# Attention with spatial reduction, then a gated feed-forward layer: a reordered prologue with larger loads, weights cast by DMA and dummy products

## Chip, cores and metric

One NeuronCore of a Trainium2 chip. The metric is device microseconds of one execution. Each kernel was run several times, with one execution profiled; the median of the runs is given.

Words used: TensorE (PE) multiplies, DVE is VectorE, ACT is ScalarE, POOL is GpSimd, SP is SyncE, which issues most loads. PEld is TensorE's loading of weights. PSUM is the memory that TensorE's products are written to; this kernel uses it in eight banks. SBUF is the memory in which the other tiles lie.

## The reference

```python
# q [4, 12288, 128], kv [4, 384, 32, 128], w_sr [128, 128]; float32
kv_pool = kv.reshape(B, H//4, 4, W//4, 4, C).mean(axis=(2, 4))   # 768 rows per image
k = v = kv_pool.reshape(B, -1, C) @ w_sr
s = (q @ k.transpose(0, 2, 1)) / sqrt(C)
a = exp(s - max);  a /= a.sum(-1, keepdims=True) + 1e-9
x = (a @ v).reshape(49152, 128)
out = (np.maximum(x @ w_gate, 0.0) * (x @ w_val)) @ w_out        # 1536 wide
```

Each of the four images gives 768 pooled rows: six **chunks** of 128. A chunk is pooled (adds over 4 lines, then over 4 columns), turned, projected by `w_sr` to keys, and turned once more to serve as values. The 49152 queries go through in 96 **tiles** of 512.

## The kernel before

The main loop runs, in one iteration, the scores of tile k, the values of tile k-1, the feed-forward products of tile k-3 and the output product of tile k-4. The keys of images 1 to 3 are made inside it, with GpSimd doing the adds. Only the first image has nothing to hide behind: its keys are made in a **prologue**, with the scores of the first four tiles beside them. These are the parts concerned.

```python
def pool_lines(eng, b, jc, other=None):             # chunk jc: 4 lines -> 1
    parts = kv_in.pop((b, jc))
    ...
    for i in range(2):                              # i == 0 on GpSimd in the prologue
        (other if i == 0 and other else eng).tensor_tensor(
            s2[:, i], parts[:, 2 * i], parts[:, 2 * i + 1], op=ALU.add)
    eng.tensor_tensor(s1, s2[:, 0], s2[:, 1], op=ALU.add)
    return s1
...
def values(k, jc, half, turn=True):
    ...                                             # 2 products of 128 x 129 (column 128: the sum)
    if jc == NJC - 1:
        ...                                         # own: the columns of this half
        nc.vector.tensor_copy(x16s[k][:, own, :], x_ps[:, :, 0:C])
        nc.vector.reciprocal(rinvs[k][:, own], x_ps[:, :, C])
        if half == 1:                               # inverse squares, used on the output
            ...                                     # rinv: the four inverses of the tile
            nc.vector.tensor_tensor(inv2s[k][:, :, 0], rinv, rinv, op=ALU.mult)
...
# prologue
for pair in range(1, NJC // 2):
    kv_load(0, pair, fine=pair == NJC // 2 - 1)     # last pair in 2 KB pieces
... # float32 weights loaded by SyncE into staging tiles
for jc in range(NJC):
    s1 = pool_lines(nc.vector, 0, jc, nc.gpsimd)
    kvT = turn_pooled(s1)                           # 4 float32 turns summed in PSUM, copy by DVE
    ...                                             # values of tile 0, chunk jc-1
    project(0, jc, kvT)                             # float32 product, copy by DVE: the keys
    ...                                             # values of tile 1, chunk jc-1
    for k in range(GRP):
        scores(k, jc)                               # product, exponential by ACT
        if k == 0:
            turn_values(0, jc)
q_load(1); q_turn(1)
for w16, w32 in staged:
    nc.gpsimd.tensor_copy(w16, w32)                 # weights cast by GpSimd
q_load(2)
...                                                 # last values of tiles 0 and 1, turn of tile 0
for k in range(LAG, last + 1):                      # main loop
    ...
```

The softmax here doesn't subtract the row's maximum and nothing guards it: scores larger than these inputs give would overflow.

## Time and profile before

| | kernel before |
|---|---|
| median of 4 runs | 1066.1 us (1065.6 to 1069.05) |
| profiled span | 1064.3 us |
| prologue, to the first feed-forward product | 46.93 us |
| first main iteration, to the first output product | 8.19 us |
| an undisturbed later tile (from its first output product to the next tile's) | 10.52 us |

The prologue is short, so averages over the span hide it. One has to cut the trace at its landmarks: the first score product of each chunk, the first feed-forward product (where TensorE becomes full), and the first output product. The prediction below does so. Two groups, with shapes kept apart, show that something disturbs the adds (columns: line, engine, operation, tiles, shapes, count, then busy us and mean ns, then idle before):

```profile
L140 DVE TENSOR_TENSOR s<-parts 128x512 f32<-128x512 f32 x6 | 6.8, 1127 | 3.6 <-DMA parts<-in_kv_dram 3.6
...
L144 DVE TENSOR_TENSOR s<-s 128x512 f32<-128x512 f32 x6 | 5.3, 883 | 0.6
```

An add of this shape takes 0.69 us when nothing disturbs it; a mean of 1127 ns over six means that some took far longer.

### The profile page before, as it was taken

What the parts mean: (1) busy time and instruction counts of PE and PEld (TensorE: products, weight loads), DVE (VectorE), ACT (ScalarE), POOL (GpSimd) and SP (SyncE); (2) the same over time, 40 slices, a digit from 0 to 9 for tenths busy, and PEclk for the clock granted to TensorE, in tenths of its full rate; (3) what the DMA queues carried; (4) which work ended last, traced back from release to release, by engine and by line L of the source; (5) the groups of instructions that cost most, each with busy time, mean ns of one, the idle gap of its engine ahead of it and who ended that gap; (6) DMA issues with size and microseconds to landing.
All of it is one profiled execution on the core that took longest, in us unless ns stands there. A gap on an engine that the chain in (4) does not pass through costs nothing.

```text
span 1064.3 us, 26131 instructions
## 1 busy us (share of the span) xinstructions
PE 1033.3 (97%) x9930; PEld 687.2 (65%) x9930; DVE 929.6 (87%) x1816; ACT 910.2 (86%) x1746; POOL 114.8 (11%) x132
## 2 busy tenths in 40 slices
PE   4699999999999999999999999999999999999997
PEld 2366666666666666666666666666666666666664
DVE  3698989998989898989898989898989898988896
ACT  3498888888888888888888888888888888888886
POOL 2200033300000004520000001530000000000000
PEclk9999999999999999999999999999999999999999
DMA  9631446422413325523132235552322332313121
GB/s 295 152 75 31 85 130 171 123 55 62 86 30 86 66 76 182 157 58 86 31 85 59 57 71 130 145 144 51 85 61 55 71 63 54 66 36 61 42 35 45
DMA packets 126574, 91.93 MB, mean 86 GB/s; under 512 B 101872, under 2 KB 103536, under 8 KB 126448
## 3 DMA queue, kind: packets, MB, share of 16 engines
q1 hardware_dynamic: 123136, 78.21, 27.7%
q0 software_dynamic: 3312, 12.06, 6.8%
q8 instruction: 77, 1.26, 0.5%
q14 instruction: 49, 0.40, 0.1%
HBM read 52.76 MB, written 25.17 MB: 73 GB/s over the span
## 4 chain that ended last, share of the span: by engine, by line
PE 96%; DVE 2%; DMA 1%; issue 0%; ACT 0%; SPq 0%; ACTq 0%; DVEq 0%
PE bank_ps L253 24%; PE bank_ps L239 23%; PE bank_ps L228 23%; PE bank_ps L198 12%; PE bank_ps L186 11%; PE bank_ps L168 1%; PE bank_ps L158 1%; DMA parts<-in_kv_dram 1%; DVE s L140 1%; DVE s L144 1%; DVE hT L242 0%; SPq L134 0%; ACT o_sb L263 0%; PE bank_ps L175 0%; DVE x L205 0%
## 5 line engine op out<-in xcount | busy, mean ns | idle before, releaser
L242 DVE SCALAR_TENSOR_TENSOR hT<-bank_ps,val 128x512 f16<-128x512 f32 x1152 | 765.2, 687 | 100.2 <-ACT val L232 70.0
L232 ACT CAST val<-bank_ps 128x512 f16<-128x512 f32 x1152 | 678.1, 589 | 120.4 <-PE bank_ps L228 117.9
L253 PEld LDWEIGHTS <-hT 128*128 128x128 f16 x4608 | 351.1, 98 | 206.0 <-DVE hT L242 2.9
L253 PE MATMUL bank_ps<-wo,hT 128*128 128x128 f16 x4608 | 443.4, 219 | 2.1 <-DVE hT L242 2.0
L228 PE MATMUL bank_ps<-xT,wv 128*128 128x512 f16 x1152 | 436.6, 379 | 1.3 <-DVE xT L223 1.3
L239 PE MATMUL bank_ps<-xT,wg 128*128 128x512 f16 x1152 | 435.7, 378 | 0.9 <-DVE hT L242 0.9
L187 ACT ACTIVATE aT<-bank_ps 128x512 f16<-128x512 f32 x576 | 345.4, 603 | 17.5 <-PE bank_ps L186 17.5
L198 PE MATMUL bank_ps<-kv,aT 128*128 128x129 f16 x2304 | 225.8, 220 | 0.1
L198 PEld LDWEIGHTS <-aT 128*128 128x128 f16 x2304 | 178.7, 98 | 70.1 <-issue 1.5
L186 PE MATMUL bank_ps<-qT,kv 128*128 128x512 f16 x576 | 217.6, 382 | 0.5 <-DVE kv L169 0.5
L239 PEld LDWEIGHTS <-wg 128*128 128x128 f16 x1152 | 111.4, 97 | 65.1
L228 PEld LDWEIGHTS <-wv 128*128 128x128 f16 x1152 | 112.7, 98 | 0.1
L205 DVE CAST x<-bank_ps 128x256 f16<-128x256 f32 x192 | 79.6, 415 | 0.7 <-PE bank_ps L198 0.7
L77 POOL DMA_DIRECT2D q<-in_q_dram x23 | 12.6, 546 | 553.6 <-DMA qT<-q 553.4
L140 POOL TENSOR_TENSOR s<-parts 128x512 f32<-128x512 f32 x42 | 52.9, 1269 | 168.1 <-DMA parts<-in_kv_dram 159.8
L265 DVE TENSOR_TENSOR o_sb<-bank_ps,inv 128x512 f32<-128x512 f32 x93 | 63.3, 681 | 0.0
L186 PEld LDWEIGHTS <-kv 128*128 128x128 f16 x576 | 56.5, 99 | 3.7 <-issue 1.6
L206 DVE RECIPROCAL rinv<-bank_ps 128x2 f32<-128x2 f32 x192 | 30.7, 160 | 0.0
L158 PE MATMUL bank_ps<-ident,s 128*128 128x128 f32 x42 | 10.0, 317 | 14.2 <-DVE s L144 14.2
L144 POOL TENSOR_TENSOR s<-s 128x512 f32<-128x512 f32 x18 | 22.8, 1268 | 1.4
L210 DVE TENSOR_TENSOR inv<-rinv 128x4 f32<-128x4 f32 x96 | 18.2, 190 | 3.3
L158 PEld LDWEIGHTS bank_ps<-ident,s 128*128 128x128 f32 x42 | 5.8, 159 | 17.3 <-DVE s L144 5.9
(33 smaller groups left out, 101.4 us busy)
## 6 DMA issues: line engine op xcount, KB each, us to landing
out_dram<-o_sb SPq DMA_DIRECT2D x96, 256.0 KB, 2.2
parts<-in_kv_dram SPq DMA_DIRECT2D x44, 512.0 KB, 6.1
q<-in_q_dram POOLq DMA_DIRECT2D x23, 512.0 KB, 5.1
parts<-in_kv_dram SPq DMA_DIRECT2D x8, 256.0 KB, 9.7
xT<-x SPq DMA_TRANSPOSE x94, 2.5
q<-in_q_dram SPq DMA_DIRECT2D x4, 256.0 KB, 7.7
w<-in_moe_w_val_dram SPq DMA_DIRECT2D x2, 384.0 KB, 7.6
w<-in_moe_w_gate_dram SPq DMA_DIRECT2D x2, 384.0 KB, 7.7
```

Source lines behind the costliest of these rows:

```text
L140: (other if i == 0 and other else eng).tensor_tensor(s2[:, i], parts[:, 2 * i], parts[:, 2 * i + 1], op=ALU.add)
L144: eng.tensor_tensor(s1, s2[:, 0], s2[:, 1], op=ALU.add)
L186: nc.tensor.matmul(s_ps, kv16[:, k // NST, jc, 0:C], qT_of(k), start=True, stop=True)
L187: nc.scalar.activation(aTs[k][:, jc, :], s_ps, AF.Exp, scale=qk_scale)
L198: nc.tensor.matmul(x_ps[:, i, :], aTs[k][:, jc, s * 128 : (s + 1) * 128], kv16[:, k // NST, jc, C : 2 * C + 1], start=(jc == 0 and i == 0) ...
L205: nc.vector.tensor_copy(x16s[k][:, own, :], x_ps[:, :, 0:C])
L228: nc.tensor.matmul(va_ps, wv16[:, fb * 128 : (fb + 1) * 128], xTs[k], start=True, stop=True)
L232: nc.scalar.copy(val, va_ps)
L239: nc.tensor.matmul(g_ps, wg16[:, fb * 128 : (fb + 1) * 128], xTs[k], start=True, stop=True)
L242: nc.vector.scalar_tensor_tensor(hTs[k][:, fb, :], g_ps, 0.0, vals.pop((k, fb)), op0=ALU.max, op1=ALU.mult)
L253: nc.tensor.matmul(o_ps[:, s, :], hTs[k][:, fb, s * 128 : (s + 1) * 128], wo16[:, fb, :], start=(fb == 0 and s == 0), stop=(fb == NFB - 1) ...
L265: nc.vector.tensor_tensor(o_sb, o_ps, inv2.to_broadcast([128, NS, 128]), op=ALU.mult)
```

## The change

Its intent is to shorten the prologue. All pieces of the first image are 4 KB; chunk jc+1 is pooled, turned and projected while the scores of chunk jc run; DVE does nearly all adds; weights come as float16 by a casting DMA; 34 dummy products run before and 34 after the first q turn, to bring TensorE to its full clock; five pairs of the value products of tile 2 move from the first main iteration into the prologue's waits, and some copies move to ScalarE.

```diff
-def kv_load(b, pair, fine=False):          # 2 KB pieces where fine
+def kv_load(b, pair):                      # 4 KB pieces (two chunks side by side)
 ...
-    staged: float32 weights by SyncE, cast later by nc.gpsimd.tensor_copy
+    idle = bank([128, 128])
+    def keep_warm(n):
+        for _ in range(n):
+            nc.tensor.matmul(idle, ident16, ident16, start=True, stop=True)
+    keep_warm(34)
     q_cast(0)
     q_turn_pe(0)
+    keep_warm(34)
 ...
+    (chunk 0: adds, turns, projection, keys; chunk 1: adds; q turns 1 to 3)
     for jc in range(NJC):
-        (adds, turns, projection, keys of chunk jc, then scores of tiles 0 to 3)
+        scores(0, jc)
+        turn_values(0, jc, nc.scalar.copy)
+        turn_pooled(0, jc + 1, ...)         # if there is one
+        for k in range(1, GRP):
+            scores(k, jc)
+        project(0, jc + 1)
+        keep_keys(0, jc + 1)
+        # even jc: four adds, for chunks jc+2 and jc+3 (one of chunk 4's on GpSimd);
+        # odd jc: the two adds left of chunk jc+2, around keep_keys
+        (values of tiles 0 and 1, chunk jc-1)
+        if jc == 2:
+            for own in (slice(0, D_FF // 2), slice(D_FF // 2, D_FF)):
+                nc.gpsimd.dma_start(wv16[:, own], moe_w_val[:, own])
+                nc.gpsimd.dma_start(wg16[:, own], moe_w_gate[:, own])
+            q_load(1); q_turn(1)
+            nc.gpsimd.dma_start(wo16, moe_w_out.rearrange("(fb f) c -> f fb c", f=128))
+            q_load(2)
+    (values of tile 2, half 0, chunks 0 to 4, ahead of the first turn of x)
```

More of the change, by code (lines that the diff above doesn't have):

```diff
@@ L88, in q_turn, with q_load_plain @@
         qTs[g] = qT
-    def q_load_plain(i):
-        q32 = work.tile([128, NS, C], FP32, tag="q32", bufs=GRP, name="q32")
+    def q_load_plain(i0, i1):
+        q32 = work.tile([128, i1 - i0, NS, C], FP32, tag=f"q32_{i0}", bufs=1, name="q32")
         nc.sync.dma_start(
-            q32, q[0, 0 : GRP * T, :].rearrange("(p i s) c -> i p s c", p=128, i=GRP)[i]
+            q32, q[0, 0 : GRP * T, :].rearrange("(p i s) c -> p i s c", p=128, i=GRP)[:, i0:i1]
         )
-        q32s[i] = q32
+        for i in range(i0, i1):
+            q32s[i] = q32[:, i - i0]
     def q_cast(i):
@@ L118, with add_lines @@
     kv_in = {}
-    def kv_load(b, pair, fine=False):
+    def kv_load(b, pair):
         parts = work.tile([128, r, 2, r, C], FP32, tag="kv_in", bufs=3)
-        lines = kv[b, pair * 2 * HC : (pair + 1) * 2 * HC]
+        rows = kv[b, pair * 2 * HC : (pair + 1) * 2 * HC].rearrange(
+            "(hp dh) (wp h dw) c -> dh hp wp (h dw c)", dh=r, h=2, dw=r
+        )
+        for dh in range(r):
+            nc.sync.dma_start(parts[:, dh].rearrange("p h dw c -> p (h dw c)"), rows[dh])
         for h in range(2):
             kv_in[b, 2 * pair + h] = parts[:, :, h]
-            rows = lines[h * HC : (h + 1) * HC].rearrange(
-                "(hp dh) (wp dw) c -> dh hp wp (dw c)", dh=r, dw=r
-            )
-            for dh in range(r if fine else 0):
-                nc.sync.dma_start(parts[:, dh, h].rearrange("p dw c -> p (dw c)"), rows[dh])
-        rows = lines.rearrange(
-            "(hp dh) (wp h dw) c -> dh hp wp (h dw c)", dh=r, h=2, dw=r
-        )
-        for dh in range(0 if fine else r):
-            nc.sync.dma_start(parts[:, dh].rearrange("p h dw c -> p (h dw c)"), rows[dh])
-    def pool_lines(eng, b, jc, other=None):
-        parts = kv_in.pop((b, jc))
-        s2 = work.tile([128, 2, r, C], FP32, tag="kv_s2")
-        for i in range(2):
-            (other if i == 0 and other else eng).tensor_tensor(
-                s2[:, i], parts[:, 2 * i], parts[:, 2 * i + 1], op=ALU.add
-            )
-        s1 = work.tile([128, r, C], FP32, tag="kv_s1")
-        eng.tensor_tensor(s1, s2[:, 0], s2[:, 1], op=ALU.add)
-        return s1
+    s2s, s1s, kv_Ts, key_banks = {}, {}, {}, {}
+    def add_lines(eng, b, jc, i):
+        if i == 0:
+            s2s[b, jc] = work.tile([128, 2, r, C], FP32, tag="kv_s2", bufs=2, name="kv_s2")
+        parts, s2 = kv_in[b, jc], s2s[b, jc]
+        if i < 2:
+            eng.tensor_tensor(s2[:, i], parts[:, 2 * i], parts[:, 2 * i + 1], op=ALU.add)
+        else:
+            s1s[b, jc] = work.tile([128, r, C], FP32, tag="kv_s1", bufs=2, name="kv_s1")
+            eng.tensor_tensor(s1s[b, jc], s2[:, 0], s2[:, 1], op=ALU.add)
+            del kv_in[b, jc], s2s[b, jc]
     def pool_columns(eng, s1):
@@ L152, in pool_columns, with turn_pooled @@
         return s3
-    def turn_pooled(pooled):
+    def turn_pooled(b, jc, pooled):
         tp = bank([128, 128])
@@ L161, in turn_pooled, with project, keep_keys, turn_values @@
             )
-        kvT = work.tile([128, 128], FP32, tag="kvT")
-        nc.vector.tensor_copy(kvT, tp)
-        return kvT
-    def project(b, jc, kvT):
-        pr = bank([128, 128])
-        nc.tensor.matmul(pr, w_sr_f32, kvT, start=True, stop=True)
+        kv_Ts[b, jc] = work.tile([128, 128], FP32, tag="kvT", name="kvT")
+        nc.vector.tensor_copy(kv_Ts[b, jc], tp)
+    def project(b, jc):
+        key_banks[b, jc] = bank([128, 128])
+        nc.tensor.matmul(key_banks[b, jc], w_sr_f32, kv_Ts.pop((b, jc)), start=True, stop=True)
+    def keep_keys(b, jc):
         nc.vector.tensor_scalar(
-            kv16[:, b, jc, 0:C], pr, 1.0 / (r * r), None, op0=ALU.mult
+            kv16[:, b, jc, 0:C], key_banks.pop((b, jc)), 1.0 / (r * r), None, op0=ALU.mult
         )
-    def turn_values(b, jc):
+    def turn_values(b, jc, copy):
         vt = bank([128, 128], FP16)
         nc.tensor.transpose(vt, kv16[:, b, jc, 0:C], ident16)
-        nc.vector.tensor_copy(kv16[:, b, jc, C : 2 * C], vt)
+        copy(kv16[:, b, jc, C : 2 * C], vt)
     aTs, x_banks, x16s, xTs, rinvs, inv2s = {}, {}, {}, {}, {}, {}
@@ L187, in scores, with values @@
         nc.scalar.activation(aTs[k][:, jc, :], s_ps, AF.Exp, scale=qk_scale)
-    def values(k, jc, half, turn=True):
+    def values(k, jc, half):
         if jc == 0:
@@ L202, in values, with keep_values, x_turn @@
             )
-        if jc == NJC - 1:
-            own = slice(2 * half, 2 * half + 2)
-            nc.vector.tensor_copy(x16s[k][:, own, :], x_ps[:, :, 0:C])
-            nc.vector.reciprocal(rinvs[k][:, own], x_ps[:, :, C])
-            if half == 1:
-                rinv = rinvs.pop(k)
-                inv2s[k] = work.tile([128, NS, 1], FP32, tag="inv2", bufs=8, name="inv2")
-                nc.vector.tensor_tensor(inv2s[k][:, :, 0], rinv, rinv, op=ALU.mult)
-            if half == 1 and turn:
-                x16 = x16s.pop(k)
-                xT = work.tile([128, NS, 128], FP16, tag="xT", bufs=5, name="xT")
-                nc.sync.dma_start_transpose(xT, x16.rearrange("p s c -> p (s c)"))
-                xTs[k] = xT.rearrange("c s p -> c (s p)")
+    def keep_values(k, half, copy=nc.vector.tensor_copy):
+        own = slice(2 * half, 2 * half + 2)
+        x_ps = x_banks.pop((k, half))
+        copy(x16s[k][:, own, :], x_ps[:, :, 0:C])
+        nc.vector.reciprocal(rinvs[k][:, own], x_ps[:, :, C])
+        if half == 1:
+            rinv = rinvs.pop(k)
+            inv2s[k] = work.tile([128, NS, 1], FP32, tag="inv2", bufs=8, name="inv2")
+            nc.vector.tensor_tensor(inv2s[k][:, :, 0], rinv, rinv, op=ALU.mult)
+    def x_turn(k):
+        x16 = x16s.pop(k)
+        xT = work.tile([128, NS, 128], FP16, tag="xT", bufs=5, name="xT")
+        nc.sync.dma_start_transpose(xT, x16.rearrange("p s c -> p (s c)"))
+        xTs[k] = xT.rearrange("c s p -> c (s p)")
     def x_turn_pe(k):
@@ L287 @@
     nc.sync.dma_start(w_sr_f32, w_sr)
-    q_load_plain(0)
+    q_load_plain(0, 1)
     kv_load(0, 0)
-    for i in range(1, GRP):
-        q_load_plain(i)
+    q_load_plain(1, GRP)
     for pair in range(1, NJC // 2):
-        kv_load(0, pair, fine=pair == NJC // 2 - 1)
+        kv_load(0, pair)
     wg16 = const.tile([128, D_FF], FP16)
@@ L297 @@
     wo16 = const.tile([128, NFB, 128], FP16)
-    HF = D_FF // 2
-    staged = []
-    w32 = work.tile([128, 2, 2, HF], FP32, tag="kv_in", bufs=3, name="w32")
-    for i in range(2):
-        own = slice(i * HF, (i + 1) * HF)
-        for n, (w16, w) in enumerate(((wv16, moe_w_val), (wg16, moe_w_gate))):
-            nc.sync.dma_start(w32[:, i, n], w[:, own])
-            staged.append((w16[:, own], w32[:, i, n]))
-    w32 = work.tile([128, NFB, 128], FP32, tag="kv_in", bufs=3, name="w32")
-    nc.sync.dma_start(w32, moe_w_out.rearrange("(fb f) c -> f fb c", f=128))
@@ L308, with pool_of @@
-    staged.append((wo16, w32))
+    def pool_of(jc):
+        return nc.gpsimd if jc == NJC - 2 else nc.vector
+    idle = bank([128, 128])
[3 more added lines that the diff above has]
+    keep_warm(34)
     q_cast(0)
     q_turn_pe(0)
-    for jc in range(NJC):
-        s1 = pool_lines(nc.vector, 0, jc, nc.gpsimd)
-        kvT = turn_pooled(s1)
-        if jc == 0:
-            for i in range(1, GRP):
-                q_cast(i)
-        else:
-            values(0, jc - 1, 0, turn=False)
-            values(0, jc - 1, 1, turn=False)
-        project(0, jc, kvT)
-        if jc == 0:
-            for i in range(1, GRP):
-                q_turn_pe(i)
-        else:
-            values(1, jc - 1, 0, turn=False)
-            values(1, jc - 1, 1, turn=False)
-        for k in range(GRP):
-            scores(k, jc)
-            if k == 0:
-                turn_values(0, jc)
@@ L333 @@
-    q_load(1)
-    q_turn(1)
-    for w16, w32 in staged:
-        nc.gpsimd.tensor_copy(w16, w32)
-    q_load(2)
-    for k in range(2):
-        for half in range(2):
-            values(k, NJC - 1, half, turn=False)
-    x_turn_pe(0)
+    keep_warm(34)
+    for i in range(1, GRP):
+        q_cast(i)
+    add_lines(nc.vector, 0, 0, 0)
+    add_lines(nc.vector, 0, 1, 0)
+    add_lines(nc.vector, 0, 0, 1)
+    add_lines(nc.vector, 0, 0, 2)
+    turn_pooled(0, 0, s1s.pop((0, 0)))
+    add_lines(nc.vector, 0, 1, 1)
@@ new lines @@
+    project(0, 0)
+    keep_keys(0, 0)
+    for i in range(1, GRP):
+        q_turn_pe(i)
+        if i == 1:
+            add_lines(nc.vector, 0, 1, 2)
+    for jc in range(NJC):
+        scores(0, jc)
+        turn_values(0, jc, nc.scalar.copy)
+        ahead = jc + 1 < NJC
+        if ahead:
+            turn_pooled(0, jc + 1, s1s.pop((0, jc + 1)))
+        for k in range(1, GRP):
+            scores(k, jc)
+        if ahead:
+            project(0, jc + 1)
+        if ahead and jc % 2 == 1:
+            add_lines(nc.vector, 0, jc + 2, 1)
+        if ahead:
+            keep_keys(0, jc + 1)
+        if jc % 2 == 1 and ahead:
+            add_lines(nc.vector, 0, jc + 2, 2)
+        elif jc + 3 < NJC:
+            add_lines(pool_of(jc + 2), 0, jc + 2, 0)
+            add_lines(nc.vector, 0, jc + 3, 0)
+            add_lines(nc.vector, 0, jc + 2, 1)
+            add_lines(nc.vector, 0, jc + 2, 2)
+        if jc > 0:
+            for k in range(2):
+                for half in range(2):
+                    values(k, jc - 1, half)
+        if jc == 2:
+            for own in (slice(0, D_FF // 2), slice(D_FF // 2, D_FF)):
+                nc.gpsimd.dma_start(wv16[:, own], moe_w_val[:, own])
+                nc.gpsimd.dma_start(wg16[:, own], moe_w_gate[:, own])
+            q_load(1)
+            q_turn(1)
+            nc.gpsimd.dma_start(wo16, moe_w_out.rearrange("(fb f) c -> f fb c", f=128))
+            q_load(2)
@@ L344 @@
+    for half in range(2):
+        values(0, NJC - 1, half)
+        keep_values(0, half)
+    for jc in range(NJC - 1):
+        values(2, jc, 0)
+    x_turn_pe(0)
+    for half in range(2):
+        values(1, NJC - 1, half)
+        keep_values(1, half, nc.scalar.copy)
+    left = [(2, NJC - 1, 0)]
+    left += [(k, jc, half) for k, half in ((3, 0), (2, 1), (3, 1)) for jc in range(NJC)]
     last = NT + LAG - 1
-    kv_s3, kv_Ts = {}, {}
+    kv_s3 = {}
     for k in range(LAG, last + 1):
@@ L360 @@
             if k == LAG:
-                for jc in (2 * i, 2 * i + 1):
-                    values(k - 1 + step % 2, jc, half)
+                own, left = left[:2], left[2:]
+                for kV, jc, half in own:
+                    values(kV, jc, half)
+                    if jc == NJC - 1:
+                        keep_values(kV, half, nc.scalar.copy)
+                        if half == 1:
+                            x_turn(kV)
             elif step % 2 == 0:
@@ L368 @@
                 values(k - 1, 2 * i + 1, half)
+                if i == NJC // 2 - 1:
+                    keep_values(k - 1, half)
+                    if half == 1:
+                        x_turn(k - 1)
             if kF < NT:
@@ L376 @@
                 if step == 3 and 0 <= at - 2 < NJC:
-                    kv_s3[b, at - 2] = pool_columns(nc.gpsimd, pool_lines(nc.gpsimd, b, at - 2))
+                    for i in range(3):
+                        add_lines(nc.gpsimd, b, at - 2, i)
+                    kv_s3[b, at - 2] = pool_columns(nc.gpsimd, s1s.pop((b, at - 2)))
                 if 0 <= at - 4 < NJC:
                     if step == 5:
-                        kv_Ts[b, at - 4] = turn_pooled(kv_s3.pop((b, at - 4)))
+                        turn_pooled(b, at - 4, kv_s3.pop((b, at - 4)))
                     if step == 7:
-                        project(b, at - 4, kv_Ts.pop((b, at - 4)))
+                        project(b, at - 4)
+                        keep_keys(b, at - 4)
                     if step == 9:
-                        turn_values(b, at - 4)
+                        turn_values(b, at - 4, nc.vector.tensor_copy)
             if k == last and step >= 2:
```

## The prediction

> **What bounds the kernel now.** I read the page first, for engine shares and the chain that ended last.
>
> ```profile
> PE 1033.3 (97%) x9930; PEld 687.2 (65%) x9930; DVE 929.6 (87%) x1816; ACT 910.2 (86%) x1746; POOL 114.8 (11%) x132
> ...
> PE 96%; DVE 2%; DMA 1%; issue 0%; ACT 0%; SPq 0%; ACTq 0%; DVEq 0%
> ```
>
> TensorE is 97% busy and 96% of the chain; busy time includes modelled ends, so I trust the chain more. Only the remaining 4% is open to a change that leaves the main loop's arithmetic alone. Next, the table of stretches, cut where each key chunk's first score product starts (columns: stretch, length, then busy us of PE, PEld, DVE, ACT, POOL, then granted clock, DMA share, GB/s).
>
> ```profile
> 12.14:16.01 3.87, 3.16 (x18) 2.43 (x19) 1.43 (x4) 1.59 (x3) 0.00 (x0) 1.00 1.03 421
> 16.01:21.62 5.61, 4.68 (x21) 2.69 (x20) 2.93 (x6) 2.11 (x4) 2.54 (x2) 1.00 1.05 288
> 21.62:26.09 4.47, 3.01 (x20) 1.71 (x19) 2.10 (x5) 2.06 (x4) 1.27 (x1) 1.00 1.06 267
> 26.09:30.29 4.20, 2.68 (x19) 1.59 (x19) 2.10 (x5) 2.06 (x4) 2.01 (x3) 1.00 1.01 350
> 30.29:38.56 8.27, 3.71 (x19) 2.39 (x20) 5.50 (x5) 2.06 (x4) 4.96 (x6) 0.85 0.84 165
> 38.56:43.03 4.47, 3.07 (x20) 1.71 (x20) 2.10 (x5) 2.06 (x4) 0.00 (x0) 0.90 1.01 178
> 43.03:46.93 3.90, 2.37 (x18) 1.10 (x18) 2.60 (x12) 2.06 (x4) 0.53 (x1) 1.00 0.46 69
> 46.93:55.29 8.36, 8.36 (x80) 5.49 (x79) 7.04 (x15) 6.85 (x12) 0.00 (x0) 1.00 0.17 33
> ...
> 900.00:910.50 10.50, 10.50 (x106) 6.96 (x104) 9.40 (x18) 9.36 (x19) 0.00 (x0) 1.00 0.14 38
> ```
>
> The prologue ends at 46.93 us, when the first feed-forward product starts. From there PE is full, 10.50 us per tile of 512 tokens, to the end. So the whole change is worth the distance by which it moves 46.93. In the prologue one chunk takes 4.2 us undisturbed, 5.61 early and 8.27 once, though no engine is busy for more than PE's 2.7 us of an undisturbed one: it is a chain of hand-overs. The waits within the first 50 us name its longest link, and the timeline from 28 to 36 us shows the 8.27.
>
> ```profile
> PE bank_ps L158 <- DVE s L144: 14.2, 6, 5.6
> ```
>
> ```profile
> 28.34 0.63 PE L158 MATMUL bank_ps<-ident,s 128*128 128x128 f32 x4 [1.11 <-DVE s L144]
> ...
> 30.29 0.39 PE L186 MATMUL bank_ps<-qT,kv 128*128 128x512 f16 x1 [0.16 <-DVE kv L169]
> ...
> 30.92 2.94 DVE L140 TENSOR_TENSOR s<-parts 128x512 f32<-128x512 f32 x1
> 30.94 0.83 POOL L336 CAST wg<-w 128x768 f16<-128x768 f32 x1
> ...
> 33.96 1.83 DVE L144 TENSOR_TENSOR s<-s 128x512 f32<-128x512 f32 x1
> ```
>
> The reader is to see two things. From pooled chunk to scores takes 1.95 us (28.34 to 30.29: four turns, copy, two-pass projection, copy), with the pooling adds before it, nothing overlapped. And the same two adds that take 0.69 us each elsewhere took 2.94 and 1.83 us while GpSimd cast weights.
>
> **What the Trainium skill says.** (1) "SBUF — State Buffer", section "Who interferes with whom": a DVE instruction with two SBUF inputs contends with a GpSimd instruction that reads SBUF, and the later one blocks. The trace agrees: 2.94 and 1.83 against 0.69 us. (2) "TensorE: Matmul & The Clock Gate", Part 1: TensorE starts at half rate, is released after a busy window of some 3.4 us and throttled again after an idle one. The trace agrees: the four turns took 1.11 us at 12.14 and 0.63 at 28.34; the clock records show half speed from 36.06 to 39.47 us, exactly 3.41, after PE's idle stretch from 31.44 to 35.94. (3) "DMA: Bandwidth & Descriptors", "Specifications", gives 512 B as enough for line rate. The trace disagrees: in the DMA view of the first 60 us (1.5 us per figure) the 4 KB pieces run at 416 to 421 GB/s, the 2 KB pieces at 255 to 291. (4) The same page, "SWDGE vs HWDGE vs iDMA": a cast during DMA can only be issued by GpSimd. The q loads already do it here, 0.55 us of GpSimd per issue.
>
> ```profile
> GB/s 0 117 199 358 385 371 352 358 421 421 416 291 255 279 284 281 258 262 393 352 321 273 182 30 46 188 157 215 104 0 106 218 25 5 0 0 0 11 87 87
> ```
>
> **The change, part by part.**
> *4 KB pieces.* By the packet records, in order of start, a 512 KB load in 4 KB pieces takes 1.25 us and the last pair's eight loads in 2 KB pieces 7.8 us (17.03 to 24.8). In 4 KB pieces they take 4 x 1.25 = 5.0; the three q loads in one (6 KB runs) take about 1.9 for 2.3. The last image line lands near 21.7 instead of 25.0, plus some 0.8 us until an engine sees it (landed 9.85, add at 10.60). But before, chunk 4 was pooled at 30.9 and chunk 5 at 39.45, long after landing: **worth nothing by itself**; it only keeps the data ahead of the new schedule.
> *Weights by DMA.* Removes five GpSimd casts (4.8 us). On the path this was (2.94 - 0.69) + (1.83 - 0.69) = 3.4 us, and the PE idleness it made cost the half clock: turns 0.99 - 0.63 and the rest of chunk 4 to the scores, together 0.7. Sum 4.1 = 8.27 - 4.2. It adds five GpSimd-issued loads after 22 us, queued with the two q loads that were GpSimd's before: four weight pieces at about 1 us each (a q load of 1 MB read took 2.6 us by its packets), so wv and wg land by about 28 and q of group 1 by about 31, turned by 39; needed at about 37 and 45. Off the path.
> *Dummies.* 34 at about 107 ns = 3.6 us from 1.7 us on, and again from 6.4 to at most 10: some eight nearly busy microseconds, enough for a whole window. PE should then be full speed at 12.1, and the gaps that follow (at most about 3 us) should keep it so. That saves about 0.5 on chunk 0's turns, 0.35 on its projection and similar on chunk 1.
> *One chunk ahead.* I laid the instructions out by hand in each engine's order with the measured durations: add 0.69 (+0.1 if dependent), turns 0.63, projection 0.46, each copy 0.29, hand-over to PE 0.15 and from PE 0.04. First adds at 8.15, 8.84, 10.60 and 11.39 as DMA allows (unchanged); turns at 12.14; keys kept at 14.1; scores of chunk 0 at 15.3, after the three remaining q turns. Chunk 1, already pooled at 15.3, has its keys at 17.7 and scores at 17.8. Then DVE does four adds, 17.74 to 20.6; turns of chunk 2 at 20.75, scores 23.05; chunk 3 at 25.95; four adds again, 25.9 to 28.1; chunk 4's scores 30.35; chunk 5's 33.5. So the cadence for a pair is still about 7.5 us, DVE plus two waits on it; overlap saves most at chunks 1 and 5. Against before: 16.01, 21.62, 26.09, 30.29, 38.56, 43.03.
> *Close of the prologue.* From chunk 5's scores to the first feed-forward product took 3.90. Scores 0.4, exponential 0.6, copy of the values now on ScalarE 0.35, last values, two casts and reciprocals on DVE 1.3, turn and copy 0.7: about 3.7. Start of the main loop: **33.5 + 3.7 = 37.2, so 9.7 us earlier**.
> *First main iteration.* Five of the 24 value pairs of products of tiles 2 and 3 have moved into PE's wait: 10 products at 0.055 = 0.55 us less of the 8.36. Their copies move to ScalarE: 4 x about 0.4 on top of 12 x 0.58; it may trail PE by a copy or two, which free banks carry.
> Sum: 9.7 + 0.55 = 10.3 us. 1066.4 - 10.3 = **1056 us**, 1.0%.
>
> **The rivals.** *The clock is not held.* If dummies fail or a gap re-throttles, every chunk pays about 1 us (turns 0.48, projection 0.34, scores 0.2): up to 6 back, 1062. For: early on PE was 75% busy (3.74 of 5 us, 15 to 20 us) and still slow until about 22. Against: dummies are denser than that. *DVE waits take the place of the casts.* Keys of the even chunks stand before the adds in DVE's order, and GpSimd's one remaining add for chunk 4 can block a DVE add by up to 1.3: perhaps 2 us, 1058. *Late weights.* wo in 512 B pieces and GpSimd's descriptor work delay q of group 1 or wv: they have 6 to 9 us of slack, so unlikely; 1060 if so. *Given back in the first iteration* by ScalarE: 1.5 at most, 1057.5. *Better than laid out:* the data is there at 22.5; if DVE's waits overlap more, the loop starts near 33: 1052. *No gain, as the main loop's bound re-absorbs it:* PE is continuous after 46.93, so an earlier start must shift the end; not credible.
>
> **Range and chances.** The rivals span 1052 to 1062; most combinations give 1053 to 1060, so I take 1052 to 1060. A gain over 2% needs 21.3 us, a main loop starting near 25.6, only 3 us after the last line can be seen with two chunks still to pool: 2%. Slower by 2% would need a fault that nothing here suggests: 1%. Within 2%: 97%.
>
> **What would show it.** Right: first feed-forward product at 35 to 39; DVE adds in the prologue all near 0.69 except one beside GpSimd; no GpSimd casts of weights; turns at 12 us take 0.63 and no half clock after; score starts at about 15, 18, 23, 26, 30, 33.5; the image loads at about 420 GB/s to 22 us; 10.5 us per later tile as before. Wrong: a turn near 1.0 us, a wait for wv or the turned q, ScalarE holding PE in the first iteration, or a per-tile time other than 10.5 (then the main loop changed and my premise fails).

## The result

| | before | after |
|---|---|---|
| median of 4 runs | 1066.1 us | 1057.78 us (1057.12 to 1059.46) |
| profiled span | 1064.3 | 1055.9 |
| first feed-forward product | 46.93 | 38.05 |
| first main iteration | 8.19 | 7.56 |
| from first output product to that of tile 92 | 963.9 | 964.9 |

Ratio 0.9919, 95% interval 0.9897 to 0.994. Ratios here are the mean time of one kernel's runs over that of the other's of the same rounds, so not quite the ratio of the medians. The time is inside the predicted range, 1.8 us above the predicted value.

The page of the changed kernel, the lines that answer to those of before:

```profile
PE 1035.0 (98%) x9998; PEld 691.4 (65%) x9998; DVE 926.2 (88%) x1809; ACT 912.2 (86%) x1758; POOL 107.1 (10%) x127
...
PE 96%; DVE 1%; ACT 1%; DMA 1%; issue 0%; SPq 0%; ACTq 0%; DVEq 0%
```

Whole-span shares hardly move. The table of stretches, cut at the same landmarks (columns as in the prediction):

```profile
12.38:16.26 3.88, 3.16 (x18) 2.43 (x19) 2.30 (x6) 1.76 (x3) 0.00 (x0) 0.50 1.03 420
16.26:19.27 3.01, 2.63 (x13) 1.69 (x12) 1.29 (x5) 1.75 (x5) 0.00 (x0) 0.70 1.03 414
19.27:25.13 5.86, 3.69 (x19) 2.62 (x20) 3.74 (x8) 2.80 (x7) 3.30 (x5) 0.71 0.54 181
25.13:27.64 2.51, 2.32 (x22) 1.54 (x20) 1.11 (x4) 1.75 (x5) 2.30 (x4) 1.00 1.04 174
27.64:31.61 3.97, 2.33 (x21) 1.55 (x19) 3.05 (x7) 2.22 (x7) 0.00 (x0) 1.00 1.01 172
31.61:34.19 2.58, 2.34 (x22) 1.55 (x20) 1.13 (x3) 2.23 (x7) 0.00 (x0) 1.00 1.50 178
34.19:38.05 3.86, 3.26 (x37) 2.16 (x36) 1.54 (x7) 3.15 (x9) 0.00 (x0) 1.00 1.25 189
38.05:45.61 7.56, 7.56 (x67) 4.73 (x68) 6.59 (x17) 6.78 (x16) 0.53 (x1) 1.00 0.69 131
900.00:910.50 10.50, 10.50 (x104) 6.98 (x102) 9.38 (x19) 9.36 (x20) 0.00 (x0) 1.00 0.28 65
```

The 8.27 us stretch is gone; chunks 4 and 5 follow at 3.97 and 2.58. But the first three stretches show granted clocks of 0.50, 0.70 and 0.71: the dummies did not keep TensorE at speed. The load rate (DMA view of the first 60 us, 1.5 us per figure) stays at 397 to 426 GB/s from 9 to 21 us; the last of the 4 KB pieces had landed at 22.97 us:

```profile
GB/s 0 104 205 369 369 391 422 397 410 426 421 410 412 407 197 0 81 191 131 166 202 178 191 221 188 184 125 0 101 210 136 89 0 0 0 11 0 72 223 215
```

Where the 8.4 us of the spans came from: 8.88 us earlier start of the main loop, 0.63 us in its first iteration, then 1.0 us *lost* between the first and the 92nd output product, and 0.1 at the end (8.88 + 0.63 - 1.01 - 0.11 = 8.39).

### Two things to follow

**The clock.** The clock records change only at steps of 3.41 us. The table of stretches, cut at these steps in the changed kernel (the first figure after the length is TensorE's busy us, the third from last is the clock):

```profile
0.99:4.40 3.41, 2.68 (x26) 2.69 (x27) 0.00 (x0) 1.23 (x2) 0.70 (x3) 1.00 0.52 123
4.40:7.81 3.41, 2.78 (x49) 2.60 (x47) 0.42 (x1) 0.62 (x1) 0.00 (x0) 1.00 0.99 371
7.81:11.23 3.42, 0.16 (x3) 0.00 (x0) 1.61 (x3) 0.00 (x0) 0.00 (x0) 1.00 1.01 410
11.23:14.64 3.41, 1.88 (x8) 1.42 (x9) 1.95 (x4) 1.14 (x2) 0.00 (x0) 0.50 1.01 411
...
18.05:21.47 3.42, 1.28 (x7) 0.59 (x5) 2.65 (x6) 2.22 (x5) 0.00 (x0) 1.00 1.01 402
21.47:24.88 3.41, 2.99 (x13) 2.25 (x14) 1.32 (x4) 1.44 (x3) 3.05 (x5) 0.50 0.22 45
```

(Before the first record the clock column reads 1.00 for want of data; the dummies' spacing of about 0.1 us in that time, 34 in 3.33 us, shows half speed.) The first batch did release the clock, at 4.40. For that reason the second batch, 34 products, took only 2.06 us and ended at 7.97. TensorE then waited 4.4 us for chunk 0; the clock fell at 11.23, before the first real product at 12.38. It came back at 18.05 and fell again at 21.47, after a window that was 1.28 us busy.

**The main loop.** Tile by tile both kernels take 10.52 us, and 0.38 more in the tiles that also turn and project a later image's chunks. But TensorE stands still for 0.3 to 0.9 us now and then: three times in the trace before, five times in the trace after (gaps between starts of products over 0.3 us, at 162, 396, 651, 673 and 695 us). One of them in the timeline:

```profile
650.05 0.16 DVE L206 RECIPROCAL rinv<-bank_ps 128x2 f32<-128x2 f32 x1
...
650.14 1.26 POOL L138 TENSOR_TENSOR kv_s<-parts 128x512 f32<-128x512 f32 x1 [1.82 <-DMA parts<-in_kv_dram]
650.24 1.19 DVE L210 TENSOR_TENSOR inv<-rinv 128x4 f32<-128x4 f32 x1
...
652.08 0.38 PE L240 MATMUL bank_ps<-xT,wg 128*128 128x512 f16 x1 [0.51 <-DVE hT L243]
```

The squaring of four numbers per partition takes 0.16 us as a rule. Here it took 1.19, ending with GpSimd's add that had begun 0.1 us before it; DVE fell behind, and TensorE waited for it. In the ten traces whose kernel does the squaring so, there are 39 such stalls, and each ends 1.2 to 2.0 us after the start of a squaring that took 0.60 us or more; no squaring that long went without one. It is the one instruction of the main loop on DVE with two inputs in SBUF. The Trainium skill, "SBUF — State Buffer", section "Who interferes with whom", says that such an instruction and a GpSimd instruction that reads SBUF exclude each other; the trace agrees.

### The profile page after: what moved, and what is told of

Read it like the earlier page. It is cut to its first block, busy times and chain, and to the rows that moved or that the text cites. A ratio compares the mean times of both kernels' runs of the same rounds, so it can differ in the third digit from the quotient of the medians.

```text
span 1055.9 us, 26244 instructions
## 1 busy us (share of the span) xinstructions
PE 1035.0 (98%) x9998; PEld 691.4 (65%) x9998; DVE 926.2 (88%) x1809; ACT 912.2 (86%) x1758; POOL 107.1 (10%) x127
## 3 DMA queue, kind: packets, MB, share of 16 engines
q8 instruction: 78, 1.28, 0.5%
## 4 chain that ended last, share of the span: by engine, by line
PE 96%; DVE 1%; ACT 1%; DMA 1%; issue 0%; SPq 0%; ACTq 0%; DVEq 0%
PE bank_ps L254 24%; PE bank_ps L240 24%; PE bank_ps L229 23%; PE bank_ps L196 12%; PE bank_ps L184 12%; DMA parts<-in_kv_dram 1%; PE bank_ps L155 1%; PE bank_ps L164 1%; DVE hT L243 0%; ACT aT L185 0%; DVE kv_s L138 0%; DVE kv_s L141 0%; SPq L127 0%; ACT o_sb L264 0%; PE bank_ps L173 0%
## 5 line engine op out<-in xcount | busy, mean ns | idle before, releaser
L205 DVE CAST x<-bank_ps 128x256 f16<-128x256 f32 x186 | 76.9, 414 | 2.1 <-PE bank_ps L196 2.1
L138 POOL TENSOR_TENSOR kv_s<-parts 128x512 f32<-128x512 f32 x37 | 46.5, 1269 | 167.7 <-DMA parts<-in_kv_dram 145.0
L141 POOL TENSOR_TENSOR kv_s<-kv_s 128x512 f32<-128x512 f32 x18 | 22.8, 1268 | 1.4
L155 PE MATMUL bank_ps<-ident,kv_s 128*128 128x128 f32 x24 | 5.2, 353 | 8.7 <-DVE kv_s L141 8.4
L146 POOL TENSOR_TENSOR s<-kv_s 128x256 f32<-128x256 f32 x18 | 13.1, 726 | 1.4
```

Source lines behind the costliest of these rows:

```text
L138: eng.tensor_tensor(s2[:, i], parts[:, 2 * i], parts[:, 2 * i + 1], op=ALU.add)
```

## The experiments

Each row was run in rounds that also ran the kernel before; the rows are from four sets of rounds, so compare rows by their ratios. The column "prologue" is from the DVE add that takes chunk 0's last lines to the first feed-forward product, so that it leaves out when the loads happened to land (this add began between 10.40 and 11.65 us). "Loop" is from the first output product to that of the 92nd tile; it and the number of stalls (gaps between product starts over 0.3 us, later than the first two iterations and before that 92nd product) are worked out from the trace's records of the products.

| run | median us (runs) | ratio to before | prologue | loop | stalls |
|---|---|---|---|---|---|
| before | 1066.1 (4) | 1 | 36.3 | 963.9 | 3 |
| after | 1057.78 (4) | 0.9919 | 27.1 | 964.9 | 5 |
| no_dummies | 1057.66 (4) | 0.9919 | 27.6 | 964.4 | 5 |
| fine_back | 1057.79 (4) | 0.9917 | 26.3 | 963.2 | 2 |
| casts_back | 1057.50 (4) | 0.9919 | 27.2 | 964.6 | 4 |
| before_dma_cast | 1066.03 (4) | 1.0011 | 31.0 | 964.5 | 5 |
| before_dma_cast_early | 1063.72 (6) | 0.9966 | 31.8 | 964.6 | 6 |
| clock_held | 1055.69 (6) | 0.9900 | 25.9 | 963.9 | 2 |
| inv_psum | 1055.91 (6) | 0.9902 | 27.5 | 962.9 | 0 |
| before_inv_psum | 1066.24 (6) | 0.9995 | 32.9 | 963.2 | 0 |
| inv_act | 1060.88 (6) | 0.9947 | 26.3 | 967.8 | 0 |
| after_again | 1057.58 (5) | 0.9919 | 27.2 | 965.2 | 5 |
| before_again | 1067.12 (5) | 1.0007 | 36.4 | 963.7 | 2 |
| held_both | 1053.97 (4) | 0.9884 | 25.4 | 962.9 | 0 |

All gave correct results.

### One part undone at a time

**no_dummies**: both calls of `keep_warm` and their bank taken out of the changed kernel.

```diff
-    keep_warm(34)
     q_cast(0)
     q_turn_pe(0)
-    keep_warm(34)
```

> The changed kernel without its 68 dummy products. In its trace the dummies brought the clock to full at 4.40 us and it fell back to half at 11.23, before the first key product at 12.38. Theory A (the dummies as written bought nothing: the second batch, at full speed, took 2.06 us and left 4.4 us of idle TensorE): the four turns of chunk 0 take 1.1 us as before, the first feed-forward product stays within 0.5 us of 38.05, the time within 1 us of 1057.8. Theory B (they are worth something, by where they put the clock's later windows): the start of the main loop moves later by 1 to 2 us, 1059 to 1060.

The time is the same. From the add of chunk 0's last lines to its first scores took 5.36 us, with dummies 5.35 (17.01 - 11.65 and 16.26 - 10.91). The prologue differs by 0.4 us, the medians by 0.1. The first feed-forward product came at 39.23, further from 38.05 than the 0.5 us that theory A allowed; 0.74 of these 1.18 us is the later landing of chunk 0's lines. As written, the dummies bought nothing in the median that can be told from noise.

Yet what they buy depends on where the clock's steps fall. Of the six traces with just these 68 dummies, chunk 0's turns took 1.11 or 1.12 us in four (after, after_again, casts_back, inv_psum; prologues of 27.1 to 27.5), and 0.65 or 0.66 in two, where the clock was still full (fine_back, inv_act; 26.3). In the changed kernel's trace the step on which it fell came at 11.23 us, before these turns; in fine_back's at 14.12, after them, though TensorE's wait was nearly as long. The line of fine_back (in brackets, that wait):

```profile
12.92 0.66 PE L160 MATMUL bank_ps<-ident,kv_s 128*128 128x128 f32 x4 [4.05 <-DVE kv_s L146]
```

**fine_back**: the last pair of the first image in 2 KB pieces.

```diff
-        kv_load(0, pair)
+        kv_load(0, pair, fine=pair == NJC // 2 - 1)
```

> The changed kernel with the last pair of chunks of the first image in 2 KB pieces again, as before. Theory A (these chunks are pooled long after they land: GpSimd's add at 21.83, DVE's at 27.5 and later): the last image line lands some 2.8 us later, the load rate falls to about 280 GB/s for it, and the first feed-forward product stays within 0.5 us of 38.05; time within 1 us of 1057.8. Theory B (the landing paces the prologue, the piece size is worth its 2.8 us): 40 to 41 and 1060.

The time is the same (1057.79), though the load rate fell to 283 to 290 GB/s (means of 3.41 us) from 17.5 us on and the last line landed at 25.77 us, 2.8 later. The prologue in its trace was even 0.8 us shorter; there the clock happened to be full for chunk 0's turns, as shown above. The piece size is worth nothing by itself, as predicted.

**casts_back**: float32 weights by SyncE and GpSimd's casts, in the new order.

```diff
-            for own in ...: nc.gpsimd.dma_start(wv16[:, own], ...); nc.gpsimd.dma_start(wg16[:, own], ...)
             q_load(1); q_turn(1)
-            nc.gpsimd.dma_start(wo16, ...)
+            for w16, w32 in staged:
+                nc.gpsimd.tensor_copy(w16, w32)
             q_load(2)
```

> The changed kernel with the weights loaded as float32 by SyncE and cast by GpSimd again, at the place where the loads now are. Theory A (GpSimd's casts block DVE adds that have two SBUF inputs): one or more adds of chunks 4 and 5 take 1.5 to 3 us instead of 0.69, and the first feed-forward product comes 1.5 to 4 us later than 38.05; time 1059 to 1062. Theory B (the adds were slow for another reason, such as the loads landing): all DVE adds stay near 0.69, time within 1 us of 1057.8.

My theory A failed: the time is that of the changed kernel. The timeline says why:

```profile
24.82 0.68 DVE L141 TENSOR_TENSOR kv_s<-kv_s 128x512 f32<-128x512 f32 x1
24.97 1.21 POOL L367 CAST wg<-w 128x768 f16<-128x768 f32 x1 [0.15 <-DMA w<-in_moe_w_gate_dram]
26.13 0.82 POOL L367 CAST wv<-w 128x768 f16<-128x768 f32 x1
26.90 0.82 POOL L367 CAST wg<-w 128x768 f16<-128x768 f32 x1
```

Here four of the five casts run from 24.0 to 27.7 us, while DVE mostly reads PSUM or waits, and the fifth from 32.14 to 33.61, as the last add ends. One of them met an add and gave way (1.21 instead of 0.82); one add took 0.87. The exclusion is real, but the new order already took the adds out of the casts' way. So the casting DMA is not needed for the gain.

### One part alone

**before_dma_cast**: the kernel before, with casting DMAs where GpSimd's casts stood (the float32 loads by SyncE go too).

```diff
     q_load(1)
     q_turn(1)
-    for w16, w32 in staged:
-        nc.gpsimd.tensor_copy(w16, w32)
+    for own in ...: nc.gpsimd.dma_start(wv16[:, own], ...); nc.gpsimd.dma_start(wg16[:, own], ...)
+    nc.gpsimd.dma_start(wo16, ...)
     q_load(2)
```

> The kernel before with one part of the change alone: weights cast by DMA, issued by GpSimd where its casts stood. Theory A (the casts cost chunk 4 its 4.1 us: 3.4 of slowed adds and 0.7 of half clock): the two adds at 30.9 take 0.69 us each, no half clock at 36, the first feed-forward product at 42.5 to 43.5 instead of 46.93, time 1061.5 to 1063. The remaining 4 to 5 us of the change are then the order of the work. Theory B (the chunk waits for something else, or the late weights now hold the first feed-forward product): gain under 2 us.

Chunk 4 took 4.20 us instead of 8.27, the two adds 0.68 and 0.69, and the main loop started at 42.22: the step is right in size. And yet the median is that of before; runs went from 1063.4 to 1070.6. The trace shows one way in which it is given back, and one that can do so in other runs. First, half clock from 42.38 to 45.79, on the first iteration, which took 9.85 us (8.19 in the trace of before). Second, the turned q of group 1: SyncE issued its DMA from 34.38, and the landing released GpSimd's next load only at 51.47 (two lines, of SyncE's and of GpSimd's timeline):

```profile
34.38 6.80 SPq L87 DMA_TRANSPOSE qT<-q  x1
```

```profile
51.47 0.54 POOL L77 DMA_DIRECT2D q<-in_q_dram  x1 [17.96 <-DMA qT<-q]
```

It is first read at 52.51, only 1 us later. In the kernel before, this wait ended at 43.78, in the changed kernel at 40.86.

**before_dma_cast_early**: the same, with the loads issued after GpSimd's add of chunk 3, and q of group 1 ahead of `wo`.

```diff
+        if jc == 3:
+            (wv and wg in halves, q_load(1), q_turn(1), wo)     # in the chunk loop
```

> The kernel before with weights cast by DMA, this time issued after GpSimd's add of chunk 3, and the q of group 1 between the weights and wo, as in the changed kernel. In the first version the main loop started at 42.22 against 46.93, but the turned q of group 1 landed near 51.4, 1 us before its use, two of four runs took 1068 to 1071, and 3.41 us of half clock fell on the first iteration. Theory A (late q of group 1, queued beside the small pieces of wo, holds the slow runs): turned q lands before 46, no run over 1066, median 1061 to 1063. Theory B (the spread is the clock's window alone): spread as wide as before, some runs at 1068 and more.

The turned q was there at 40.34, no run was above 1064.1, and the median is 1063.72, 2.2 us (0.34%) under before in its rounds. The spread of the late version went with the late q; none of its slow runs was profiled, so that the q itself held them is argued, not shown. The early version's runs fall in two groups, 1061 (two) and 1063.6 to 1064.1 (four); the profiled one, of the second group, had half clock from 43.04 to 46.45 and a first iteration of 9.79 us. Of theory A's signs two came (q before 46, no run over 1066), and the median is 0.7 us above its range: it fits the worst runs. That the clock's window parts the two groups is not shown, since the faster group was not profiled.

### The clock

**clock_held**: more dummies, placed where TensorE waits.

```diff
-    keep_warm(34)                                   # after q_turn_pe(0)
+    keep_warm(96)
...
 def turn_pooled(b, jc, pooled, warm=0):
     tp = bank([128, 128])
+    for _ in range(warm):                           # 30 before chunk 2's turns, 22 before chunk 4's
+        nc.tensor.matmul(tp, ident16, ident16, start=True, stop=True)
```

> The changed kernel with more dummies: 96 instead of 34 after the first q turn, to reach from 5.9 to about 11.5 us, and 30 and 22 of them, written into the bank of the next chunk's turns, ahead of the turns of chunks 2 and 4 where TensorE waits for DVE. Theory A (the clock fell in those gaps and its half speed is the 0.7 to 2.1 us by which the score starts trail my layout): no half clock between 5 and 1040 us, turns of chunk 0 and 2 take 0.63, scores start near 15.4, 18, 23.2, 26, 30.3, 33, the first feed-forward product at 36.7 to 37.4, time 1056.5 to 1057.2. Theory B (the half clock is hidden behind DVE's adds): start within 0.3 us of 38.05.

Start of the main loop 37.02, prologue 25.9 for 27.1, median 1055.69, some 2 us under the changed kernel (1.3 us of it is prologue; the trace also happened to have three stalls fewer). Chunk 0's turns took 0.66 us and chunk 2's too. So theory A held for the start. The changed kernel was not in these rounds and the intervals of the two ratios overlap (0.9876 to 0.9924, and 0.9897 to 0.994), so the 2 us are confirmed only by held_both below. Against theory A's "no half clock", one window still fell:

```profile
11.93:15.34 3.41, 1.94 (x14) 1.17 (x14) 2.29 (x6) 1.56 (x3) 0.00 (x0) 1.00 1.02 413
15.34:18.75 3.41, 3.17 (x15) 2.19 (x15) 1.59 (x4) 1.65 (x5) 0.00 (x0) 0.50 1.03 414
```

1.94 us of 3.41 busy was not enough there.

### The stalls

**inv_psum** and **before_inv_psum**: no DVE instruction of the main loop reads two operands from SBUF; the same edit on either kernel.

```diff
-        nc.vector.reciprocal(rinvs[k][:, own], x_ps[:, :, C])
+        nc.vector.tensor_copy(rinvs[k][:, own], x_ps[:, :, C])
+        nc.vector.tensor_tensor(                    # one input SBUF, one PSUM
+            rinvs[k][:, own], rinvs[k][:, own], x_ps[:, :, C], op=ALU.mult)
         ...
-            nc.vector.tensor_tensor(inv2s[k][:, :, 0], rinv, rinv, op=ALU.mult)
+            nc.vector.reciprocal(inv2s[k][:, :, 0], rinv)
```

> The changed kernel with the inverse squares formed without a DVE instruction that has two SBUF inputs: copy of the sums, product of the copy with the sums in PSUM, one reciprocal. In the changed kernel's trace TensorE stands still five times in the main loop (0.5 to 0.9 us) and each time the small squaring of the inverses took about 1 us instead of 0.16 beside a GpSimd add; three times in the kernel before. Theory A (that is the collision): no such DVE instruction over 0.3 us, no gap of TensorE over 0.3 us in the main loop before its tail, 1.5 to 3 us less than 1057.8. Theory B (the stalls come from the image loads or buffers): stalls remain, time unchanged or longer by two more small DVE instructions per tile.

> The same edit on the kernel before. Theory A (the collisions fall by chance of timing on either kernel, and took about 1 us of the change's gain away): 1 to 2 us less than before, 1064 to 1065, and the spans of this run and of the changed kernel with the same edit differ by 9.3 to 9.8 us, the distance between their starts of the second main iteration (55.12 against 45.61), instead of 8.4. Theory B: the difference stays at 8.4.

On the changed kernel theory A held: no stall in the main loop past its first two iterations; the loop took 962.9 us instead of 964.9; median 1055.91, 1.9 us less (again in other rounds, with overlapping intervals), and runs within 1.4 us of each other (1055.15 to 1056.5), although DVE does two more small instructions per tile. On the kernel before the loop fell to 963.2 without stalls in the main loop, but the median did not move by more than noise (0.9995, interval 0.997 to 1.0021), and the difference of the two spans was 5.3 us, not 9.3 to 9.8. So there my number failed. The profiled run of it was a lucky one in the prologue: this time GpSimd's casts gave way as well (two took 1.20 and 1.28 us for 0.83), DVE's adds of chunk 4 took only 1.42 and 1.12, and the clock never fell. What decides who waits there isn't shown. Its other runs, 1064.8 to 1067.9, were not profiled. What the edit is worth on the kernel before is left open; with loops of 962.9 and 963.2, the main loops of both kernels are alike once the collisions are gone.

**inv_act**: the squaring by ScalarE.

```diff
-            nc.vector.tensor_tensor(inv2s[k][:, :, 0], rinv, rinv, op=ALU.mult)
+            nc.scalar.activation(inv2s[k][:, :, 0], rinv, AF.Square)
```

> The changed kernel with the inverses squared on ScalarE instead of DVE, one small instruction per tile. Theory A: as with the version through PSUM, no collision, 1.5 to 3 us less than 1057.8, if the function needs no reload of its table. Theory B: ScalarE, 86% busy, or table reloads make it slower than 1057.8.

No collision and no table reload (one load in the trace, at the start), but slower: 1060.88. A tile took 10.57 us instead of 10.52, and the loop 967.8 us. ScalarE stands in line behind DVE's reciprocal (84 waits in the main loop, 65.9 us in all), and the copies behind it come later. So removing the collisions by a new dependence between two busy engines cost more than the collisions; that the waits are the cause is read from this trace, not tested apart.

### The spread, and both together

> The changed kernel itself, in the same rounds, to measure the spread: if the collisions of the small squaring with GpSimd's adds and the clock's window decide what differs between runs, the number of TensorE gaps in the main loop differs from the five of the first trace by one or more, the main loop from first to 92nd output product lies between 962.9 and 965, and the time between 1056.5 and 1059.5. If it repeats exactly, the stalls belong to the schedule and not to chance.

The changed kernel again: five stalls, but at other times (184, 397, 418, 440 and 653 us), prologue 27.2, loop 965.2, runs from 1056.0 to 1059.8. So the number did not differ, as had been expected, and the loop lies just above the expected 962.9 to 965; but it is not an exact repeat either. Where the stalls fall changes from run to run. Both traces of the changed kernel have five and both of the kernel before fewer (3 and 2): how much of that is chance and how much the new order's timing is not shown.

> The kernel before itself, profiled again: its runs went from 1060.6 to 1069.7. Theory A (the casts' collision with chunk 4's adds, the clock's windows and the small squaring fall differently from run to run): the two adds take other times than 2.94 and 1.83 us (1.42 and 1.12 in the variant with another squaring), or another number of half-clock windows, and the start of the main loop moves by a microsecond or more from 46.93, in step with the span. Theory B: prologue as in the first trace to 0.3 us, the spread lies elsewhere.

Two slow adds of chunk 4, as in the first trace:

```profile
31.21 2.95 DVE L140 TENSOR_TENSOR s<-parts 128x512 f32<-128x512 f32 x1
...
34.27 1.77 DVE L144 TENSOR_TENSOR s<-s 128x512 f32<-128x512 f32 x1
```

The prologue is the same to 0.1 us (36.4), so this part of theory A failed: the large collision was there in both traces of this kernel, and smaller in the variant's. What differed is the clock: a half-speed window fell on the first main iteration, 47.60 to 51.02, which then took 9.79 us instead of 8.19. The span was 1066.8 for 1064.3; that iteration is 1.6 of the 2.5 us.

**held_both**: clock_held with 106 dummies instead of 96 and 6 ahead of chunk 0's projection, and inv_psum.

> Changed kernel with both findings: dummies that hold the clock (106 after the first q turn, 6 ahead of chunk 0's projection, 30 and 22 ahead of the turns of chunks 2 and 4) and inverse squares without two SBUF inputs. If the two gains are independent (1.0 us of prologue, 1.9 us of main-loop stalls against the changed kernel's traces; medians 1055.7 and 1055.9 for one each): no half clock from 5 to 1040 us, first feed-forward product 25.2 to 25.9 us after the add that takes chunk 0's last lines (27.1 in the changed kernel), no gap of TensorE over 0.3 us in the main loop outside the first iterations, 1053.5 to 1054.5 us. If the clock's windows still fall (the 3.41 us from 11.93 was only 1.94 us busy with the first set of dummies) or the additional DVE work costs: 1055.5 or more.

Median 1053.97, ratio 0.9884 (0.9872 to 0.9897); against the changed kernel in the same rounds 3.7 us (0.35%) less, about the sum of the two. The windows of its prologue:

```profile
10.38:13.79 3.41, 3.36 (x53) 3.18 (x51) 2.03 (x4) 1.14 (x2) 0.00 (x0) 1.00 1.02 411
13.79:17.20 3.41, 2.62 (x25) 1.76 (x23) 2.64 (x9) 2.20 (x5) 0.00 (x0) 1.00 1.02 416
```

The clock stayed at full from 6.97 us to 1048.04. Score starts at 15.20, 17.34, 22.13, 25.44, 29.35 and 31.92, main loop at 35.98. This is the fastest version found, and its runs lie within 0.8 us.

## Why the prediction was right, and where it was not

1. **The premise held.** The change is worth what it moves the start of the full TensorE stretch; a later undisturbed tile takes 10.52 us in both kernels. Start moved by 8.88 us, time by 8.3.
2. **4 KB pieces, "worth nothing by itself": right** (fine_back).
3. **Weights by DMA, 4.1 us: right for the old order, but not a term of this sum.** Alone it does take chunk 4 from 8.27 to 4.20 us (before_dma_cast). In the new order the casts do no harm (casts_back), so the change without it brings the whole 9.2 us of prologue (36.3 to 27.1): the two parts overlap instead of adding up. Pieces, dummies and casts were each undone alone, never together, and the new order never ran by itself; that it alone brings the 9.2 us is therefore argued, and what in it does (a chunk ahead, adds moved from GpSimd to DVE, the rest) was not parted. My sum came out because I read the start from a layout of the whole order, not from adding the parts. That late weights and q might delay the loop I held unlikely; in the changed kernel it did not happen, in the old order the turned q landed 1.6 us before its use.
4. **Dummies: the step that failed**, "the gaps that follow (at most about 3 us) should keep it so". The gap was 4.4 us, because the dummies sped themselves up: I counted the second batch as up to 10 us at half speed, and it ended at 7.97. And an idle window is not needed: windows 1.28 us busy also ended at half clock. I had given this rival up to 6 us; it cost 1.2 to 1.7 (prologue 27.1; 25.9 in clock_held and 25.4 in held_both). That DVE's adds cover the rest is argued. Score starts trailed the layout:

| chunk | 0 | 1 | 2 | 3 | 4 | 5 | first feed-forward product |
|---|---|---|---|---|---|---|---|
| layout | 15.3 | 17.8 | 23.05 | 25.95 | 30.35 | 33.5 | 37.2 |
| after | 16.26 | 19.27 | 25.13 | 27.64 | 31.61 | 34.19 | 38.05 |
| held_both | 15.20 | 17.34 | 22.13 | 25.44 | 29.35 | 31.92 | 35.98 |

   The delay grows to 2.1 us while the clock is low and shrinks to 0.7 after. Some 0.3 us of it is the loads' landing (10.91 for 10.60). With the clock held the layout is met, and beaten by some 1.2 us: it was too slow by about that much, and this hid part of what the clock cost. That the start came within 0.85 us of the forecast is partly luck.
5. **Close of the prologue, 3.7: measured 3.86. First iteration, 0.55 less: measured 0.63.** ScalarE did not hold it. Right, though the parts listed for the close add up to 3.35, and the 8.36 us was cut at 55.29 where the first output product starts at 55.12 (8.19).
6. **A term was missing: stalls in the main loop.** I took the loop as fixed. Its length depends on how often the small squaring meets a GpSimd add: 1.0 us more in the trace after than in the trace before (1.5 in the second traces). Removing the cause took 1.9 us from the changed kernel's loop (inv_psum).

Three readings were off without harm. The last image line landed at 27.54 us before and 22.97 after by the landing records, not at 25.0 and 21.7; chunk 5's adds in the changed kernel began at 27.5. "Elsewhere" the adds did not all take 0.69 us: chunk 1's first took 1.09 beside a GpSimd add. And 10.50 is the length at which the tile's stretch was cut.

So the 1.8 us between 1056 and 1057.8 are about 0.85 of a later start and 1.0 of stalls, with 0.1 gained in the first iteration.

## What to carry to other kernels

Where one engine is full from some point to the end, measure a prologue change at that point, and then check that the distance is still there at the end. Size dummy products in time, at the speed that they themselves bring about: here the clock stayed full only when they reached up to the next real product and filled the later waits too (held_both, one trace). A tiny instruction with two SBUF inputs on a busy DVE beside GpSimd adds left gaps of up to 0.96 us in TensorE's work when it collided; with one PSUM input there were none, and handing it to another busy engine was worse than the collisions.

## What the Trainium skill lacked or had wrong

- "TensorE: Matmul & The Clock Gate", Part 1, lets the clock fall after an idle window of some 3.4 us. It also tells of a kernel whose short idle times made the clock oscillate, but not how busy a window has to be. In the first 60 us of the 14 traces here, cut at the clock's steps of 3.41 us: windows at full clock that were busy for 1.53 us (fine_back) or less all ended at half clock, and those of 1.95 us (before_again) or more all kept it. Between the two both occur: 1.58 (fine_back) and 1.82 (before) kept it, 1.88 (before_again) and 1.94 (clock_held) did not. Windows at half clock that were busy for 2.85 us (casts_back) or more ended at full clock, those of 2.63 or less did not; 2.68 did in the changed kernel, 2.74 (before) and 2.77 (no_dummies) did not. So the borders are not sharp in the profile's busy measure, whose ends are modelled.
- "DMA: Bandwidth & Descriptors", "Specifications", takes 512 B as enough for line rate. Loads here ran at 283 to 290 GB/s in 2 KB pieces (fine_back) and at 397 to 426 mostly in 4 KB pieces (after).
- The same page has no figure for a DMA transpose beside a casting load of small pieces: from issue to landing the first turn of q took 16.6 us in before_dma_cast, where it was issued 2.5 us after the load of `wo`, 7.3 us in the kernel before, and 6.6 in the changed kernel.
- "SBUF — State Buffer", "Who interferes with whom", is confirmed for the squaring: 128x4 elements, 0.16 us alone, took up to 1.27 us (before_dma_cast), about as long as the GpSimd add beside it. Its rule that issue order decides who blocks does not explain all, as far as the starts in a trace show that order: in the kernel before, the add of chunk 4 that began at 30.92 us took until 33.86, past casts that began after it, at 30.94, 31.71 and 32.49; in before_inv_psum two such casts gave way to the add instead (1.20 and 1.28 us for 0.83).
